# Attention's scores with its products, and its transposes by pairs, in two visits in place of four

## The chip, the cores and the metric

One core of a Trainium2 chip runs the whole program. The metric is the device time of one execution in microseconds, from runs of the same kernel on the chip. The kernel before takes 1135.18 us, the median of 3 runs (1135.1 to 1136.02).

## What is computed

Three stages stand behind each other. Attention has 4 batches, 8 heads, 576 tokens, 64 elements a head, and a window of 128 tokens. Its output, 2304 tokens of 512, goes through a dense layer of 2048 (softplus), and then through a mixture of 8 experts, two for each token.

```python
scores = scale * np.matmul(q, k.transpose(0, 1, 3, 2))
mask = (rel >= 0) & (rel < window)            # window 128
scores = np.where(mask, scores + bias[None], -1000000000.0)
attn = np.exp(scores - np.max(scores, axis=-1, keepdims=True))
attn = attn / (np.sum(attn, axis=-1, keepdims=True) + 1e-09)
x = np.matmul(attn, v)                        # to [2304, 512]
h = x @ w_in
x = (np.maximum(h, 0.0) + np.log1p(np.exp(-np.abs(h)))) @ w_out
# then: top 2 of 8 experts by noisy logits, relu(x @ w1[e]) @ w2[e], weighted sum
```

## The kernel before

**Tiling.** Attention works on 20 units u, five in each batch, of 128 query tokens (the fifth has 64). A unit has 4 head pairs; head pair m runs from 0 to 79 over all units (u = m // 4). The keys of a unit are its own block and the one before, 256 columns where both are there. The dense layer works on 9 chunks of 256 tokens; a chunk needs the products of all units that reach into it.

**The three steps of attention.** `step_a(m0)` (from line 327, scores) makes the scores of head pairs m0 and m0 + 1, that is two pairs of heads: 8 plain f32 matmuls of 64 rows, into two PSUM tiles, one for each of the two heads of a pair. VectorE then adds the bias and reduces each of the four blocks (L350), ScalarE takes the exponential (L356), VectorE the reciprocal of the sums (L361, L362), and GpSimd multiplies by it (L371; early on ScalarE does half of that). The tile "s" has 6 buffers, one for each head pair. The first PSUM tile is free with the third of the four reductions, the second with the fourth. `step_b(m)` (from L378) transposes the weights of one head pair on TensorE (4 transposes into one PSUM tile, L201) and copies them to "pT", on VectorE for an even m (L400), on ScalarE for an odd one (L398). `step_c(m0)` (from L405, products with values) makes the products of two head pairs, 16 plain f32 matmuls into one PSUM tile; ScalarE copies them out rounded (L430), VectorE takes the rest (L435), into the chunk's "xh" and "xl". Below, A, B and C stand for these three steps.

**PSUM.** A, B and C all take their tiles by `ps_t` (L182) from one ring with the tag "t" of 4 slots: two for A, one for each B, one for C. While the second layer's sums of chunk 1 are open (their tiles are called "z"), `few_t` (L176) sets `nt` to 2: z holds two slots and the ring has two. `part_evac` of chunk 1 gives them back.

**The dense layer between.** `mm1` makes one group of 128 of the 2048 for a chunk, 12 matmuls into "h"; softplus takes ScalarE, VectorE and GpSimd; three jobs later `mm2` makes 6 matmuls into "y" (or "z"). Both are rounded-f32 matmuls (L190). A weight is converted on the way, by ScalarE, VectorE and GpSimd (`w_convert`), its load issued by SP.

**What sets the order.** All engines take their instructions in the order in which they are written. TensorE's order is written out by hand; the other engines' instructions are set in by a planner (`Order`) with a cost for each. The lead-in calls `attn_step` for the steps below `attn_until(0)` before the first job. Then each job t calls `side_work` (L1310) twice, behind `mm1` and behind `mm2`: these calls are the gaps. `pieces_of(c)` (L1297) yields the pieces that chunk c + 1 needs, and `side_work` takes so many of them that `fed` reaches `total * gap // gaps`. A chunk of 6 jobs has 10 such gaps; chunk 1 is made in the first three jobs, chunk 2 in the next nine with 16 gaps. What is left is done when the next chunk begins. Step s gives A(s) for an even s, B(s - 3), and for an odd s C(s - 5). Loads of q and k for unit u + 2 stand ahead of step 4u + 1, that of v for unit u ahead of step 4u.

Of the kernel before, what the change touches and what calls it, by code (L numbers as in the profile page):

```python
# [25 lines left out]
class Order:  # L26
# [60 lines left out]
    def mark(self, key):  # L87
        self.done(key, self.now)
# [24 lines left out]
def moe_chain_kernel(ctx, tc, qk, v, w_in, w_out, w_gate, w_noise, noise, w1, w2, out):  # L113
# [160 lines left out]
    NM = 4 * NU  # L274
# [32 lines left out]
    def attn_load_v(u):  # L307
        b, i, q0, nq = units[u]
        r = U[u] = {}

        def load():
            r["v"] = tl(att, [P, H, D], F32, "rawv", 3, ("ce", 4 * min(NU - 1, u + 1) + 3))
            SP.dma_start(r["v"][:nq], v[b, q0:q0 + nq])
        dma(load, ("rawv", u))
# [63 lines left out]
    def step_b(m):  # L378
        u, hp = divmod(m, 4)
        b, i, q0, nq = units[u]  # L380
        m_ = M[m]
        need(("a", m))
        blocks = key_blocks(u)[0]
        nb = len(blocks)
        pt = ps_t(("b", m, len(blocks) - 1 if nq < P else 0), idle="y").rearrange("p (h b t) -> p h b t", h=2, b=2)
        for j in range(2):
            for kb, (c0, nk, vu) in enumerate(blocks):
                tr(pt[:nk, j, kb, :nq], m_["s"][:nq, j, c0:c0 + nk], ident[:nq, :nq])
        mark(("be", m))
        ph = tl(att, [P, 2, 2, P], F32, "pT", 4, ("ce", m))  # L390
        if nb == 2 and blocks[0][1] == blocks[1][1]:
            parts = [(slice(0, P), slice(0, 2))]
        else:
            parts = [(slice(0, blocks[kb][1]), slice(kb, kb + 1)) for kb in range(nb)]
        for x, (pp, kb) in enumerate(parts):
            w = 2 * nq * (kb.stop - kb.start)
            if m % 2:
                ev = ("A", ca(w), lambda pp=pp, kb=kb: ACT.activation(ph[pp, :, kb, :nq], pt[pp, :, kb, :nq], AF.Copy))  # L398
            else:
                ev = ("V", cv(w), lambda pp=pp, kb=kb: DVE.tensor_copy(ph[pp, :, kb, :nq], pt[pp, :, kb, :nq]))  # L400
            chain(ev + (("b", m, x),))
        m_["nb"] = len(parts)
        m_["pT"] = ph
# [35 lines left out]
        del M[m0], M[m0 + 1]  # L439

    LB, LC = 3, 4

    def attn_step(s):
        u = s // 4
        if s % 4 == 1 and u + 2 < NU:
            attn_load_qk(u + 2)
        if s and s % 4 == 0 and u < NU:
            attn_load_v(u)
        pieces = []
        if s < NM and s % 2 == 0:  # L450
            pieces.append(lambda: step_a(s))
        if 0 <= s - LB < NM:
            pieces.append(lambda: step_b(s - LB))
        if 0 <= s - LC - 1 < NM and (s - LC) % 2:
            pieces.append(lambda: step_c(s - LC - 1))
        return pieces

    def attn_last(c):
        return max(u for u in range(NU) if units[u][0] * S + units[u][2] < CT * (c + 1))

    def attn_until(c):
        return 4 * attn_last(c) + 3 + LC + 1

# [829 lines left out]
    NT = len(jobs)  # L1295

    def pieces_of(c):  # L1297
        for s in range(attn_until(c), attn_until(c + 1)):
            yield from attn_step(s)

    starts = {0: (0, NLEAD), NLEAD: (1, 2 * NA - NLEAD)}
    for c in range(2, NCH):
# [2 lines left out]
    feed, fed, total, gap, gaps = None, 0, 0, 0, 1  # L1305
# [37 lines left out]
    for t in range(NT + max(L2, len(items) + 2)):  # L1343
# [11 lines left out]
        if t in starts:  # L1355
            c, n = starts[t]
            if feed is not None:
                for p in feed:
                    p()
            feed = pieces_of(c) if c + 1 < NCH else None  # L1360
            total = 2 * (attn_until(c + 1) - attn_until(c)) if feed else 0
            fed, gap, gaps = 0, 0, 2 * n - 2
        if t == last_start - (NF - NA):
            open_p2()
# [7 lines left out]
        if t < NT:  # L1372
            c, fc = jobs[t]
# [17 lines left out]
        if 0 <= t - L2 < NT:  # L1391
            c, fc = jobs[t - L2]
# [74 lines left out]
```

## Time and profile before

| | us |
|---|---|
| median of 3 runs | 1135.18 |
| the profiled execution | 1135.73 |
| its span, first to last instruction | 1134.0 |
| TensorE busy | 1072.4 |
| VectorE busy | 723.6 |
| ScalarE busy | 616.8 |
| GpSimd busy | 581.7 |

The profile is one execution. PE is TensorE, DVE VectorE, ACT ScalarE, POOL GpSimd, SP SyncE, which issues most of the DMAs; SPq is its queue. PEclk is the granted clock of TensorE as a share of full speed: 1.00 is 2.4 GHz, 0.50 is 1.2 GHz. A row of the timeline merges like instructions that follow each other: its start, its length, engine, line, operation, out<-in, how many, and in brackets the idle time of the engine before it with what ended it. Starts are exact; the ends of matmuls are modelled, so spacings are read from start to start.

### The profile page before, as it was taken

To read this page: it belongs to the slowest core of one execution; us is meant where nothing else is said; L and a number is where in the kernel's file an instruction comes from. 1 tells how busy PE (TensorE), PEld (TensorE's weight loads), DVE (VectorE), ACT (ScalarE), POOL (GpSimd) and SP (SyncE) were. 2 spreads that over 40 slices of the span, in tenths; PEclk is the share of its full clock that TensorE was granted. 3 is DMA by queue.
4 is the path that set the end of the run, shared out by engine and by line. 5 is a ranking of instruction groups with operands and counts; after the bars stand their busy time and mean duration, and the time that the engine had idled before them with its cause. 6 is when DMAs were issued, how large, how long until landed. Compare 5 with 4: busy or idle time off the path is not lost.

```text
span 1134.0 us, 21375 instructions
## 1 busy us (share of the span) xinstructions
PE 1072.4 (95%) x7021; PEld 913.2 (81%) x7021; DVE 723.6 (64%) x1946; ACT 616.8 (54%) x1459; POOL 581.7 (51%) x933
## 2 busy tenths in 40 slices
PE   5599999999999999999998997999999999999997
PEld 3377777777789888888887796997997997999984
DVE  8975788889764666666767685653653653665520
ACT  7876768877764444444453543553553553555521
POOL 4576779889886676777775232222222223222112
PEclk8899999999999999999998998999999999999999
DMA  7231553555683322211348729788888888888723
GB/s 306 102 93 57 182 183 118 196 209 176 204 302 124 102 75 75 76 51 62 122 140 304 239 28 337 207 234 262 223 234 264 228 228 253 250 227 233 213 57 38
DMA packets 96561, 198.94 MB, mean 175 GB/s; under 512 B 34048, under 2 KB 44800, under 8 KB 96448
## 3 DMA queue, kind: packets, MB, share of 16 engines
q1 hardware_dynamic: 86112, 176.01, 47.3%
q0 software_dynamic: 10336, 21.54, 9.7%
q8 instruction: 56, 0.92, 0.4%
q14 instruction: 57, 0.47, 0.2%
HBM read 157.82 MB, written 39.69 MB: 174 GB/s over the span
## 4 chain that ended last, share of the span: by engine, by line
PE 65%; DVE 4%; DMA 4%; POOL 3%; ACT 2%; issue 2%; SPq 1%; DVEq 0%; POOLq 0%; ACTq 0%
PE h L190 31%; PE y L190 21%; PE z L190 9%; PE t L201 3%; PE t L190 1%; DMA rawp<-in_moe_w 1%; POOL sl L555 1%; POOL su L555 1%; DVE wlo L1154 1%; DMA rk<-rect 1%; ACT s L356 1%; DMA raw<-in_moe_w_out 1%; DVE gl L587 0%; DMA out<-ys,rc 0%; DMA x1buf<-x 0%
## 5 line engine op out<-in xcount | busy, mean ns | idle before, releaser
L190 PE MATMUL h<-xh,w 128*128 128x256 f32 x1152 | 239.6, 291 | 5.0 <-DVE sl L583 5.0
L1264 POOL DMA_INDIRECT out<-ys,rc x41 | 83.7, 2042 | 272.3 <-DVE ys L1273 131.6
L1154 DVE TENSOR_TENSOR wlo<-rawp,whi 128x1024 fp32r<-128x1024 f32 x107 | 130.8, 1222 | 136.2 <-ACT whi L1156 129.9
L190 PEld LDWEIGHTS h<-xh,w 128*128 128x128 f32 x1152 | 191.2, 193 | 19.2 <-DVE sl L583 9.5
L1156 ACT ACTIVATE whi<-rawp 128x1024 fp32r<-128x1024 f32 x107 | 113.4, 1060 | 151.2 <-PE h L190 108.1
L555 POOL TENSOR_TENSOR su<-sa,su 128x128 f32<-128x128 f32 x288 | 137.2, 497 | 86.1 <-DVE su L588 73.0
L190 PE MATMUL y<-w,gh 128*128 128x512 f32 x552 | 179.8, 407 | 0.0
L190 PE MATMUL h<-xh,whi 128*128 128x256 f32 x576 | 165.5, 287 | 6.4 <-DVE gl L1203 6.4
L190 PE MATMUL h<-xl,w 128*128 128x256 f32 x576 | 164.4, 285 | 1.1 <-DVE xl L435 1.1
L190 PE MATMUL h<-xl,whi 128*128 128x256 f32 x576 | 163.3, 283 | 0.0
L190 PE MATMUL h<-xh,wlo 128*128 128x256 f32 x576 | 163.2, 283 | 0.0
L580 ACT ACTIVATE sa<-h 128x256 f32<-128x256 f32 x144 | 54.8, 381 | 152.7 <-PE h L190 99.6
L555 POOL TENSOR_TENSOR sl<-sl,su 128x128 f32<-128x128 f32 x288 | 134.5, 488 | 3.9 <-DVE sl L583 2.8
L190 PEld LDWEIGHTS h<-xh,whi 128*128 128x128 f32 x576 | 110.1, 191 | 14.0 <-DVE gl L1203 6.8
L190 PEld LDWEIGHTS h<-xl,whi 128*128 128x128 f32 x576 | 110.2, 191 | 7.1 <-issue 1.4
L190 PEld LDWEIGHTS h<-xl,w 128*128 128x128 f32 x576 | 111.4, 193 | 4.5 <-DVE xl L435 1.6
L190 PEld LDWEIGHTS h<-xh,wlo 128*128 128x128 f32 x576 | 110.2, 191 | 0.0
L190 PE MATMUL y<-w,gl 128*128 128x512 f32 x276 | 108.7, 394 | 0.0
L190 PEld LDWEIGHTS y<-w,gh 128*128 128x128 f32 x552 | 95.3, 192 | 16.3 <-issue 2.7
L371 POOL TENSOR_TENSOR s<-s,st 128x256 f32<-128x256 f32 (+2 forms) x144 | 91.9, 661 | 25.6 <-DVE st L362 14.0
L1063 POOL DMA_INDIRECT xg<-x1buf,rc x41 | 43.2, 1054 | 106.6 <-DVE rc L1052 60.4
L587 DVE TENSOR_TENSOR gl<-sl,gh 128x256 fp32r<-128x256 f32 x144 | 76.6, 533 | 13.3 <-ACT gh L585 10.5
(256 smaller groups left out, 2265.0 us busy)
## 6 DMA issues: line engine op xcount, KB each, us to landing
rawp<-in_moe_w SPq DMA_DIRECT2D x140, 512.0 KB
raw<-in_moe_w SPq DMA_DIRECT2D x44, 512.0 KB
qkT<-in_qk SPq DMA_DIRECT2D x20, 512.0 KB
raw<-in_moe_w_in SPq DMA_DIRECT2D x16, 512.0 KB
raw<-in_moe_w_out SPq DMA_DIRECT2D x16, 512.0 KB
out<-zero SPq DMA_DIRECT2D x19, 256.0 KB
xspill<-xh SPq DMA_DIRECT2D x9, 512.0 KB
xspill<-xl SPq DMA_DIRECT2D x9, 512.0 KB
```

The costliest lines, as they stand in the source:

```text
L190: PE.matmul(o, l, r, start=start, stop=stop)
L201: PE.transpose(o, i, idn)
L356: ACT.activation(s[:nq, j, :n], s[:nq, j, :n], AF.Exp, bias=st[:nq, 0, y], scale=-1.0, accum_out=st[:nq, 1, y])
L371: POOL.tensor_tensor(s[:nq, j, :n], s[:nq, j, :n], st[:nq, 3, 2 * x + j:2 * x + j + 1].to_broadcast([nq, n]), OP.mult)
L555: POOL.tensor_tensor(o[:, z], x[:, z], y[:, z], op)
L580: chain(("A", ca(CT), lambda: ACT.activation(a, ph, AF.Abs)), ("A", ca(CT), lambda: ACT.activation(a, a, AF.Exp, scale=-1.0), ("e", t)), ( ...
L587: ("V", cv(CT), lambda: DVE.tensor_sub(gl, l, f32(gh)), ("g", t)))
L1063: POOL.indirect_dma_start(out=x, out_offset=None, in_=x1buf[:T - 3 * CT if g < NEARLY else TPAD, :], in_offset=bass.IndirectOffsetOnAxis(a ...
L1154: DVE.tensor_sub(lo, t, f32(hi))
L1156: chain(("A", ca(1024), lambda: ACT.activation(hi, t, AF.Copy), None, (("r2", j),)), ("V", cv(1024), low, ("w2", j)))
L1264: POOL.indirect_dma_start(out=out[:, :], out_offset=bass.IndirectOffsetOnAxis(ap=rc[:, a, 0:1], axis=0), in_=ys, in_offset=None, compute_o ...
```

## The change

The feeder's pieces are made anew. One piece, `products(s)`, now does A(s) and then all C up to head pair s - 6, and after that the loads that stood ahead of steps s and s + 1. The other piece does all B up to s - 3, which are two of them. So for two head pairs the feeder has two pieces in place of four (A, B, B, C). `sofar` keeps how far B and C have come. `attn_until(c)` is larger by 2 for every chunk but the first, since C of the same pairs is one step later; `pieces_of` goes by two steps, and `total` counts half as many pieces. The lead-in still goes by `attn_step`, whose pieces are now always two or three, some of them without work.

```diff
     LB, LC = 3, 4
-
-    def attn_step(s):
+    sofar = [0, 0]
+
+    def loads(s):
         u = s // 4
         if s % 4 == 1 and u + 2 < NU:
             attn_load_qk(u + 2)
         if s and s % 4 == 0 and u < NU:
             attn_load_v(u)
+
+    def b_upto(m):
+        while sofar[0] <= min(m, NM - 1):
+            step_b(sofar[0])
+            sofar[0] += 1
+
+    def c_upto(m):
+        while sofar[1] <= min(m, NM - 1):
+            step_c(sofar[1])
+            sofar[1] += 2
+
+    def attn_step(s):
+        loads(s)
         pieces = []
         if s < NM and s % 2 == 0:
             pieces.append(lambda: step_a(s))
-        if 0 <= s - LB < NM:
-            pieces.append(lambda: step_b(s - LB))
-        if 0 <= s - LC - 1 < NM and (s - LC) % 2:
-            pieces.append(lambda: step_c(s - LC - 1))
+        pieces.append(lambda: b_upto(s - LB))
+        pieces.append(lambda: c_upto(s - LC - 1))
         return pieces
+
+    def products(s):
+        if s < NM:
+            step_a(s)
+        c_upto(s - 6)
+        loads(s)
+        loads(s + 1)
+
+    def attn_pieces(s):
+        return [lambda: products(s), lambda: b_upto(s - 3)]
 
     def attn_until(c):
-        return 4 * attn_last(c) + 3 + LC + 1
+        return 4 * attn_last(c) + (10 if c else 8)
...
     def pieces_of(c):
-        for s in range(attn_until(c), attn_until(c + 1)):
-            yield from attn_step(s)
+        for s in range(attn_until(c), attn_until(c + 1), 2):
+            yield from attn_pieces(s)
...
-            total = 2 * (attn_until(c + 1) - attn_until(c)) if feed else 0
+            total = attn_until(c + 1) - attn_until(c) if feed else 0
```

## Rows read from the trace of the kernel before

**Rows 1.** The page's head: the span.
```profile
span 1134.0 us, 21375 instructions
```

**Rows 2.** Windows: stretch, length, engines' busy us (instructions), PEclk, DMA share, GB/s.
```profile
41.00:72.00 31.00, 23.56 (x181) 17.82 (x178) 28.58 (x80) 24.89 (x71) 21.74 (x32) 0.84 0.36 127
72.00:132.00 60.00, 57.21 (x441) 46.29 (x440) 37.78 (x143) 41.68 (x138) 39.15 (x81) 1.00 0.34 111
132.00:305.00 173.00, 166.28 (x1278) 131.54 (x1277) 151.93 (x447) 134.59 (x419) 151.58 (x264) 0.98 0.51 175
305.00:1134.00 829.00, 805.74 (x5013) 704.27 (x5011) 470.15 (x1168) 384.71 (x746) 351.28 (x525) 0.99 0.61 180
```

**Rows 3.** TensorE's waits, 88 to 305 us: total us, times, longest.
```profile
PE t L190 <- ACT pT L398: 2.3, 1, 2.3
PE t L201 <- DVE st L350: 2.3, 2, 1.3
PE t L190 <- DVE st L350: 2.2, 2, 1.4
PE t L201 <- POOL s L371: 1.4, 3, 0.7
```

**Rows 4.** TensorE's timeline, 209 to 217 us: start, us, instruction, shapes, count.
```profile
209.06 0.28 PE L190 MATMUL h<-xl,w 128*128 128x256 f32 x1
209.18 0.28 PE L190 MATMUL h<-xh,w 128*128 128x256 f32 x1
209.29 0.63 PE L190 MATMUL y<-w,gh 128*128 128x512 f32 x2
...
212.00 0.28 PE L190 MATMUL h<-xh,w 128*128 128x256 f32 x1
212.21 1.08 PE L339 MATMUL t<-qkT 64*64 64x256 f32 x8
...
215.63 1.09 PE L190 MATMUL t<-pT,rawv 128*64 128x128 f32 x16
216.66 0.39 PE L190 MATMUL h<-xh,w 128*128 128x256 f32 x1
216.88 0.28 PE L190 MATMUL h<-xl,w 128*128 128x256 f32 x1
```

**Rows 5.** TensorE's timeline where products are followed by scores, 222 us.
```profile
222.72 1.09 PE L190 MATMUL t<-pT,rawv 128*64 128x128 f32 x16
223.75 0.71 PE L339 MATMUL t<-qkT 64*128 64x128 f32 x8
```

**Rows 6.** TensorE's timeline, transposes behind scores with two slots, 98 and 127 us.
```profile
98.64 1.13 PE L339 MATMUL t<-qkT 64*128 64x256 f32 x8
101.07 0.63 PE L201 MATMUL t<-ident,s 128*128 128x128 f32 x4 [1.30 <-DVE st L350]
...
127.68 0.63 PE L201 MATMUL t<-ident,s 128*128 128x128 f32 x4 [0.96 <-DVE st L350]
```

**Rows 7.** VectorE's timeline behind the scores of 98.64 us: first and third reduction.
```profile
99.80 0.42 DVE L350 CUSTOM_DVE_ANT_0 s<-t,relh 128x256 f32<-128x256 f32 x1 [0.63 <-PE t L339]
...
100.49 0.42 DVE L350 CUSTOM_DVE_ANT_0 s<-t,relh 128x256 f32<-128x256 f32 x1
```

**Rows 8.** TensorE's timeline, the products that waited for a copy, and the next scores.
```profile
168.86 0.44 PE L190 MATMUL t<-pT,rawv 128*64 128x128 f32 x4 [2.33 <-ACT pT L398]
...
171.15 2.08 PE L339 MATMUL t<-qkT 64*128 64x256 f32 x8
```

**Rows 9.** Windows of 5 us in which the granted clock was low.
```profile
170.00:175.00 5.00, 5.00 (x24) 3.75 (x24) 4.00 (x15) 3.87 (x15) 4.95 (x9) 0.66 0.10 42
225.00:230.00 5.00, 4.04 (x36) 3.01 (x35) 4.04 (x19) 4.30 (x17) 5.00 (x10) 0.85 0.94 352
230.00:235.00 5.00, 5.00 (x36) 3.94 (x34) 4.93 (x14) 3.37 (x12) 3.13 (x8) 0.81 0.22 90
```

**Rows 10.** SP's own queue, 72 to 305 us: waits of the loads of v.
```profile
SPq L313 <- PE t L190: 39.9, 5, 11.6
```

## The prediction

> **What bounds the kernel now.** I read the page first for the span [rows 1], then the stretches of the run [rows 2]. TensorE is busy nearly all of the time from 72 us on. In 41 to 72 us it is not: VectorE is the full engine there (28.6 of 31 us). The changed code runs from 42 us to about 304 us, where attention's work for the next chunk is threaded between the first layer's matmuls ("h") and the second layer's ("y", for a while "z"). In 132 to 305 us TensorE idles only 6.7 of 173 us, VectorE and GpSimd being 88% busy [rows 2]. After 305 us nothing of the change runs; that stretch waits on its own work and moves as one block with whatever is won or lost before.
>
> So two things count: what TensorE does beside useful columns at the edges of attention's visits, and its waits. Its list of waits for 88 to 305 us [rows 3] holds transposes waiting for GpSimd's normalised scores (1.4 us), products waiting for the copied transposes (2.3), and transposes or products waiting for VectorE's reductions of the scores, that is for a free PSUM slot (2.3 and 2.2).
>
> **Edges.** Attention's scores (A) and products with values (C) are plain f32 matmuls. In the PE timeline [rows 4] an h matmul follows an h matmul after 0.12 us and y follows h after 0.11, but scores follow h after 0.21; behind products the first h takes 0.22 to its successor. So a run of A or C between other work costs about 0.10 at each end, 0.20 in all. Where products are followed directly by scores [rows 5] the products take 1.03 us up to the scores, as they do up to h [rows 4] (216.66 less 215.63, from the same listing), so A and C side by side share one run. How many runs there are follows from the feeder: a chunk's pieces are spread over gaps by integer division. Before, four visits per two pairs of heads come in the order A, B, B, C (B: transposes), in 10 gaps for 16 pieces (24 in two chunks). After, 8 (12) pieces: A with C, then both B. Writing both sequences out from the code, I get 57 runs of A or C behind the third h group before and 32 after: 25 fewer, 25 x 0.20 = 5.0 us. In 14 of the old runs scores meet transposes; I count that end at half, an estimate: 14 x 0.05 = 0.7 less. **Term 1: -4.3 us** (bounds -5.0 and 0).
>
> The Trainium skill speaks against this term ("TensorE: Matmul & The Clock Gate", Step-by-step: what each phase is for): the draining of one matmul overlaps the filling by the next, so that a stream is spaced by its columns. The trace agrees from h to y and not from h to A.
>
> **The stretch with two PSUM slots.** Between the z tiles' first use (about 87.7 us) and their copy (about 133 us) attention has two slots in place of four. Scores take both, so whatever takes a slot next waits for VectorE. Before, that is a B directly behind A, twice: 1.30 us and 0.96 us [rows 6]. VectorE starts its reductions 0.03 us after the last score matmul, and the third, which frees the first slot, starts 0.69 us after the first and ends a little before the transposes start [rows 7]. In the other old visits an h or y group covers this. After, C stands directly behind A in every product visit, and by the feeder's arithmetic five such visits (A 28 to 36 with C 22 to 30) fall into this stretch. What is queued behind the waiting C on TensorE is the next h or y and with it ScalarE's first pass over h; nothing else covers it. I take 1.2 each, between the two rows: 6.0 less the 2.3 that goes. **Term 2: +3.7 us** (bounds 5 x 0.96 - 2.3 = +2.5, and 5 x 2.3 - 2.3 = +9 if VectorE is a conversion step behind, the longest wait on the list).
>
> **Longer lead.** A pair's transposes now come 2.5 pair periods behind its scores, not 1.5. GpSimd's normalisation gets that much longer, so the 1.4 us of waits go; with them goes the low clock behind them, 0.85 and 0.81 granted over two stretches of 5 us [rows 9], 5 x 0.15 + 5 x 0.19 = 1.7 us. **Term 3: -3.1 us** (bounds -3.1 and 0).
>
> Products now have an h or y group and A (1.0 us) between them and their pair's second B, where some had 1.4 us and one more B. The 2.33 us wait for ScalarE's copy at 168.86 [rows 8] has ScalarE standing behind a late weight conversion, which the change doesn't touch, but the copy moves ahead of it. The scores after that wait took 2.08 us, at a granted clock of 0.66 in the stretch [rows 8, 9]: 5 x 0.34 = 1.7. I count half of 2.3 + 1.7. **Term 4: -2.0 us** (bounds -4.0 and +2, since another wait can meet the same late copy).
>
> Waits of C for reductions with four slots (2.2 us, [rows 3]) came about 2.4 us behind A. Now C no longer needs the slot of its own visit's scores; the second B does, behind C, an h or y group and one B, about 3.0 us. **Term 5: -1.0 us** (bounds -2.2 and +2).
>
> **What comes in exchange.** Reductions and the copies of the products stand in one burst on VectorE, and in one chunk two visits hold A, C and both B together, where the second B comes 1.5 us behind A, just what the reductions took on a free VectorE and more than they leave on a full one: 0.5 us each. VectorE and GpSimd do the same work in a shorter time: 152 us in some 165, 92%. A wait of one more engine queue, 1.5 us in all, is my estimate from the sum of the small waits now listed. **Term 6: +2.5 us** (bounds 0 and +8, where all gains come back as waits).
>
> **The start.** In the lead-in the steps are called one by one with the same lags, so nothing moves; empty pieces only let the weight conversion look once more. Up to the second chunk's first h group one more A and one more pair of B are to be done (about 1.3 us of TensorE, and four short reductions), taken from later. VectorE is full there; but transposes wait there for GpSimd too. I take 0 (bounds -2.5 and +1.5).
>
> **Loads.** The loads of q, k and v are still one unit and two units ahead of their use, now in the same visit behind A and C. On SP a load of v waits for old products on TensorE (39.9 us in five cases [rows 10]), with weight loads and spills queued behind it. It is emitted behind the same C as before, q and k right behind v instead of one visit later. I cost this at nothing: the products use v two visits on. If that cover goes, the price is a conversion's late weights, as in term 4.
>
> **Sum.** -4.3 + 3.7 - 3.1 - 2.0 - 1.0 + 2.5 = -4.2 us. The profiled execution took 1135.73 us (span 1134.0 and 1.7 around it), 0.55 above the median of 1135.18. From the median: **1131.0 us**.
>
> **The rivals.**
> 1. All waits named in terms 3 to 5 vanish and none comes: -4.3 + 3.7 - 3.1 - 4.0 - 2.2 = -9.9, 1125.3 us. For it speaks the longer lead everywhere; against it that these waits came from queues that other work fills.
> 2. VectorE and GpSimd become the bound: the gains reappear as waits on reductions, "sl" and "s". Term 6 is +6 to +8, the time 1134.5 to 1136.5. For: 88% busy now, GpSimd full in one of the 5 us stretches [rows 9]. Against: VectorE has a tenth of the stretch left even then, and TensorE idles so little there now.
> 3. Slower: the two slots. If VectorE is behind at each A, the wait is 2.3 us, not 1.2, and costs the clock too: of the waits seen, 1.30 left the clock full and 2.33 didn't, so the mechanism decides between these two. 5 x (2.3 + 1.7) - 2.3 = +17.7 in place of +3.7: 1145 us. Against: VectorE is 63% busy in 72 to 132 us [rows 2].
> 4. An edge between kinds costs nothing, what is seen being the end of a modelled matmul: term 1 is 0, and the change does on TensorE nothing of what it reorders for: +0.1, 1135.3 us. The page cited above would have it so. Against: starts, not ends, carry the 0.21.
>
> **How the numbers follow.** Forecast 0.48 (its own range 1127 to 1135), rival 1 0.14, rival 2 0.14, rival 3 0.16, rival 4 0.08. About 0.2%, 2.3 us, is what a measurement of this kernel can tell from no change. Faster than 1132.9: 0.8 of the forecast (0.38), all of rival 1, a little of rival 2 (0.03): 0.55. Slower than 1137.5: rival 3 and about a quarter of rival 2 and of the forecast's upper end: 0.20. The rest, 0.25, is the same. The range leaves out the low end of rival 1 and most of rival 3: 1123 to 1140.
>
> **What would show it.** Runs of A and C: scores next to products in the PE timeline, each A with C about 2.3 us from edge to edge. Term 2: five waits of C for reductions between 88 and 133 us, 1 to 1.3 us each; if there are none, or if they are over 2 us, the term is wrong. Term 3: no transposes waiting for "s" on GpSimd behind 72 us. Term 4: no product waiting for "pT". Term 6: more idle time of TensorE for reductions or "sl" than now. If the 829 us behind 305 us change in length by over 1 us, the block doesn't move as one, and the forecast fails for a reason not in it.

## The result

The changed kernel takes 1146.87 us, the median of four runs (1146.31 to 1147.63), the kernel before 1135.6 in four runs. The ratio is 1.0105 [1.0088, 1.0121]: slower by 11 to 12 us, where 1131.0 was forecast and 1140 was the end of the range. The profiled execution took 1146.31 us; its span stands against [rows 1], its stretches against [rows 2]. The page's head, kernel after:

```profile
span 1144.5 us, 21362 instructions
```

Windows of the kernel after (columns as in [rows 2]):

```profile
72.00:132.00 60.00, 53.77 (x417) 43.71 (x416) 35.04 (x131) 39.63 (x130) 39.75 (x82) 1.00 0.33 104
132.00:305.00 173.00, 160.89 (x1229) 130.60 (x1230) 148.56 (x438) 129.89 (x407) 144.97 (x251) 0.95 0.50 171
305.00:1144.00 839.00, 815.05 (x5088) 712.34 (x5086) 477.00 (x1182) 390.73 (x763) 355.35 (x537) 0.99 0.61 180
```

TensorE is idle 6.2 us in 72 to 132 us (before 2.8), and 12.1 us in 132 to 305 (before 6.7), and in the latter its granted clock is 0.95 in place of 0.98. VectorE is less busy than before in both (35.0 and 148.6 us for 37.8 and 151.9), GpSimd as busy in the first (39.8 for 39.2) and less in the second (145.0 for 151.6); part of this is that the kernel after, being late, has done less by 305 us. What TensorE waits for, in 75 to 135 us and then in 135 to 310 us of the kernel after (columns as in [rows 3]):

```profile
PE t L190 <- DVE st L350: 7.6, 5, 2.4
...
PE t L190 <- DVE pT L400: 4.8, 3, 1.9
PE t L339 <- DVE xl L435: 3.2, 1, 3.2
PE t L201 <- DVE st L350: 1.8, 2, 1.5
PE t L201 <- POOL sl L577: 0.6, 1, 0.6
```

Against [rows 3] no wait is put down to GpSimd's "s" any more. The 0.6 us that transposes wait for "sl" (at 235.92) is probably one all the same: they read nothing of "sl", and GpSimd finished two multiplications of "s" directly ahead of it (233.93 to 235.41). Products (L190 into t) wait five times for a slot, three times for copies on VectorE, and once the scores (L339) wait.

Where the time is lost can be read from the starts of the h groups, which are the same work in the same order in all kernels of this study. The table gives how much later than in the kernel before each stretch made its kernel; the marks in the kernel before are the 4th h group at 71.2 us, the 19th at 147.6, the 25th at 179.2, the 48th at 305.6, and the end of the span at 1134.0. The two-slot stretch lies in the second column.

| kernel | to 4th h | to 19th | to 25th | to 48th | to the end | sum | that run's time, us | median | ratio to before |
|---|---|---|---|---|---|---|---|---|---|
| after | +2.0 | +3.4 | +2.7 | +0.6 | +1.9 | +10.6 | 1146.3 | 1146.9 | 1.0105 [1.0088, 1.0121] |
| e1 pads stored later | +1.5 | +3.4 | -3.7 | +2.6 | +1.7 | +5.4 | 1141.1 | 1139.6 | 1.0037 [1.0023, 1.0051] |
| e2 the same, kernel before | +1.9 | 0.0 | -2.9 | +1.4 | -2.6 | -2.2 | 1133.5 | 1134.7 | 0.9996 [0.9984, 1.0008] |
| e3 C ahead of A | +6.4 | +3.7 | +2.9 | +6.8 | +1.4 | +21.2 | 1156.9 | 1160.2 | 1.0235 [1.0213, 1.0256] |
| e4 A, C apart with two slots | +1.7 | +0.3 | +0.8 | -3.6 | +0.8 | 0.0 | 1135.8 | 1139.9 | 1.0054 [1.0034, 1.0073] |
| e5 e1 and e4 | +1.5 | +0.3 | -3.7 | +2.6 | +1.5 | +2.3 | 1138.1 | 1136.1 | 1.0010 [0.9998, 1.0021] |
| e6 e5, old start | +0.6 | +2.3 | -3.7 | +2.4 | +1.6 | +3.2 | 1139.0 | 1139.7 | 1.0046 [1.0033, 1.0059] |
| e7 e5, C two head pairs later | +1.4 | +0.3 | -0.4 | -4.7 | -1.6 | -5.0 | 1130.7 | 1133.0 | 0.9985 [0.9975, 0.9996] |
| e8 e1, A, C apart | +1.5 | +0.3 | -2.7 | -2.2 | +2.1 | -1.1 | 1134.6 | 1131.6 | 0.9971 [0.9959, 0.9982] |
| e9 copies on ScalarE | -3.2 | +3.4 | -0.9 | -3.3 | -1.8 | -5.8 | 1130.0 | 1132.1 | 0.9981 [0.9967, 0.9995] |
| e10 A, C apart | +0.8 | +0.3 | -2.3 | -3.1 | -1.7 | -6.0 | 1129.9 | 1132.3 | 0.9974 [0.9964, 0.9983] |
| e11 e8, C two head pairs later | +1.9 | +0.3 | +2.0 | -5.3 | +0.2 | -1.0 | 1134.7 | 1134.6 | 0.9990 [0.9981, 1.0000] |
| e12 A, B, B, C, same lags | +1.5 | +1.3 | -1.1 | +0.8 | -0.5 | +2.0 | 1137.7 | 1137.4 | 1.0017 [1.0004, 1.0029] |
| e13 before, copies on ScalarE | -0.9 | +0.9 | +1.3 | +3.5 | -1.7 | +3.0 | 1138.8 | 1139.9 | 1.0039 [1.0025, 1.0054] |
| e14 e10, copies on ScalarE | -0.4 | +1.3 | -2.3 | -5.4 | +0.6 | -6.1 | 1129.6 | 1129.0 | 0.9934 [0.9921, 0.9948] |
| e15 A with C, B one by one | +1.8 | +3.1 | +2.7 | -3.7 | -0.9 | +3.0 | 1138.7 | 1140.3 | 1.0054 [1.0037, 1.0072] |
| e16 e14, A with C from chunk 4 on | -0.9 | +0.9 | -0.8 | -3.3 | -2.4 | -6.5 | 1129.2 | 1131.3 | 0.9964 [0.9951, 0.9978] |

The stretches are of one profiled run each, the ratios of all runs; where the two differ (e3, e4 and e8, by 3 us or more) the ratio decides. The stretch to the end moves by -2.6 to +2.1 though none of the changed code runs there, so two kernels' sums can lie over 4 us apart without a cause. The stretch to the 4th h group is of the same kind: e2 has the order of the kernel before up to there and is 1.9 us late, at a granted clock of 0.66 in 68 to 73 us (before 1.00). Of the +2.0 of the kernel after, 0.8 is there at 22.5 us already (21.7 before), in the lead-in, and e10 with the same lead-in doesn't have it; the rest is about the 1.3 us of scores and transposes that it does early.

### The profile page after: what moved, and what is told of

The parts are those of the page before. It is cut to its first block, busy times and chain, and to the rows that moved or that the text cites. A ratio compares the mean times of both kernels' runs of the same rounds, so it can differ in the third digit from the quotient of the medians.

```text
span 1144.5 us, 21362 instructions
## 1 busy us (share of the span) xinstructions
PE 1074.6 (94%) x7021; PEld 918.1 (80%) x7021; DVE 724.7 (63%) x1946; ACT 616.4 (54%) x1459; POOL 578.9 (51%) x933
## 4 chain that ended last, share of the span: by engine, by line
PE 77%; DVE 12%; POOL 3%; issue 2%; DMA 2%; ACT 2%; SPq 1%; DVEq 0%; POOLq 0%; ACTq 0%
PE h L190 35%; PE y L190 23%; PE z L190 9%; PE t L201 4%; PE t L190 3%; DVE s L350 2%; PE t L339 2%; DVE cva L519 1%; DVE cva L518 1%; DVE gl L609 1%; POOL sl L577 1%; DVE cva L517 1%; DVE w L533 1%; DVE su L610 1%; POOL su L577 1%
## 5 line engine op out<-in xcount | busy, mean ns | idle before, releaser
L190 PE MATMUL h<-xh,w 128*128 128x256 f32 x1152 | 238.5, 290 | 6.1 <-DVE sl L605 6.1
L190 PEld LDWEIGHTS h<-xh,w 128*128 128x128 f32 x1152 | 190.8, 193 | 18.1 <-DVE sl L605 11.2
L190 PE MATMUL y<-w,gh 128*128 128x512 f32 x552 | 179.6, 407 | 0.0
L190 PE MATMUL h<-xh,whi 128*128 128x256 f32 x576 | 165.6, 288 | 6.5 <-DVE gl L1225 6.5
L190 PE MATMUL h<-xl,w 128*128 128x256 f32 x576 | 164.1, 285 | 1.2 <-DVE xl L435 1.2
L190 PE MATMUL h<-xl,whi 128*128 128x256 f32 x576 | 163.4, 284 | 0.0
L190 PE MATMUL h<-xh,wlo 128*128 128x256 f32 x576 | 163.4, 284 | 0.0
L190 PEld LDWEIGHTS h<-xh,whi 128*128 128x128 f32 x576 | 110.4, 192 | 14.2 <-DVE gl L1225 6.9
L190 PEld LDWEIGHTS h<-xl,whi 128*128 128x128 f32 x576 | 110.4, 192 | 7.1 <-issue 1.4
L190 PEld LDWEIGHTS h<-xl,w 128*128 128x128 f32 x576 | 111.3, 193 | 4.5 <-DVE xl L435 1.4
L190 PEld LDWEIGHTS h<-xh,wlo 128*128 128x128 f32 x576 | 110.4, 192 | 0.0
L190 PE MATMUL y<-w,gl 128*128 128x512 f32 x276 | 109.2, 396 | 0.6 <-DVE gl L609 0.6
L190 PEld LDWEIGHTS y<-w,gh 128*128 128x128 f32 x552 | 95.8, 192 | 15.0 <-issue 1.7
L356 ACT ACTIVATE s<-s,st 128x256 f32<-128x256 f32 (+2 forms) x160 | 76.0, 477 | 21.8 <-DVE st L350 21.7
```

What stands on the lines that cost most here:

```text
L190: PE.matmul(o, l, r, start=start, stop=stop)
L356: ACT.activation(s[:nq, j, :n], s[:nq, j, :n], AF.Exp, bias=st[:nq, 0, y], scale=-1.0, accum_out=st[:nq, 1, y])
```

## Where the time went in the kernel after

**The slots.** TensorE's timeline, kernel after: scores, and behind them the products of the same visit, with two PSUM slots (the first and the last of the five):

```profile
95.36 1.14 PE L339 MATMUL t<-qkT 64*128 64x256 f32 x8
97.80 0.66 PE L190 MATMUL t<-pT,rawv 128*64 128x128 f32 x8 [1.30 <-DVE st L350]
...
129.95 1.08 PE L339 MATMUL t<-qkT 64*64 64x256 f32 x8
133.41 0.84 PE L190 MATMUL t<-pT,rawv 128*64 128x128 f32 x11 [2.38 <-DVE st L350]
```

VectorE's timeline at the same two places, kernel after: the third reduction, which frees the first slot, and at the second place the conversion and the first reduction too.

```profile
97.22 0.42 DVE L350 CUSTOM_DVE_ANT_0 s<-t,relh 128x256 f32<-128x256 f32 x1
...
131.41 0.82 DVE L519 SCALAR_TENSOR_TENSOR cva<-raw,cva 128x512 int32<-128x512 int32 x1
132.16 0.41 DVE L350 CUSTOM_DVE_ANT_0 s<-t,relh 64x256 f32<-64x256 f32 x1
...
132.84 0.41 DVE L350 CUSTOM_DVE_ANT_0 s<-t,relh 64x256 f32<-64x256 f32 x1
```

At 95.36 VectorE is free when the scores end, and the wait is 1.30 us all the same, as in the first four of the five: three reductions in a row, then the slot. At 129.95 VectorE is in a weight conversion, the reductions begin at 132.16, and the wait is 2.38.

**The late load.** SP's queue waits in 150 to 180 us, kernel after, the one that counts:

```profile
SPq L266 <- DVE pad L263: 13.9, 1, 13.9
```

SP's timeline behind that wait, kernel after:

```profile
166.36 1.79 SPq L266 DMA_DIRECT2D rect<-pad  x4
168.25 0.39 SPq L313 DMA_DIRECT2D rawv<-in_v  x1
168.69 0.45 SPq L304 DMA_DIRECT2D qkT<-in_qk  x1
169.19 0.43 SPq L505 DMA_DIRECT2D raw<-in_moe_w_in  x1
```

ScalarE's timeline, where it waits for that load, kernel after:

```profile
175.60 0.66 ACT L509 ACTIVATE cva<-raw 128x512 f32<-128x512 f32 x1 [5.92 <-DMA raw<-in_moe_w_in]
...
176.47 0.37 ACT L430 ACTIVATE xh<-t 128x256 fp32r<-128x256 f32 x1
```

TensorE's timeline, where the scores of the next visit wait, kernel after:

```profile
177.40 2.07 PE L339 MATMUL t<-qkT 64*128 64x256 f32 x6 [3.23 <-DVE xl L435]
179.41 1.12 PE L190 MATMUL t<-pT,rawv 128*64 128x128 f32 x8
```

Read them upward. Scores wait for a slot that holds old products; these products are copied by ScalarE (L430) and VectorE (L435); ScalarE stands 5.92 us in its queue for a weight that SP issued at 169.19; and SP had stood 13.9 us in front of four small stores ("pad") whose data VectorE made late, and then issued v and q, k ahead of the weight.

The order behind the stores is the change's own doing. In e10 (below), where A and C are apart, SP issues the weight directly behind them, as it does before (161.77) and in e12 (164.76). SP's timeline, e10:

```profile
160.09 1.80 SPq L266 DMA_DIRECT2D rect<-pad  x4
161.93 0.44 SPq L517 DMA_DIRECT2D raw<-in_moe_w_in  x1
162.47 0.40 SPq L313 DMA_DIRECT2D rawv<-in_v  x1
```

ScalarE then waits 3.99, 1.80 and 4.37 us for the weight (before, e10, e12), and 5.92, 5.33 and 6.38 us in the kernel after, e4 and e15, where v and q, k go first. In e9 they go first too, with a wait of 3.78.

**The copies.** TensorE's timeline, kernel after, at the first of three places where products wait for VectorE's copy of the transposes:

```profile
196.09 1.13 PE L339 MATMUL t<-qkT 64*128 64x256 f32 x8
198.81 1.09 PE L190 MATMUL t<-pT,rawv 128*64 128x128 f32 x16 [1.59 <-DVE pT L400]
```

VectorE's timeline ahead of that copy, kernel after:

```profile
195.25 0.44 DVE L517 TENSOR_SCALAR cva<-cva 128x512 f32<-128x512 f32 x1
...
196.33 0.98 DVE L519 SCALAR_TENSOR_TENSOR cva<-raw,cva 128x512 int32<-128x512 int32 x1
197.24 0.83 DVE L609 TENSOR_TENSOR gl<-sl,gh 128x256 fp32r<-128x256 f32 x1
197.99 0.68 DVE L400 COPY pT<-t 128x512 f32<-128x512 f32 x1
```

The copy stands behind a conversion and a pass of softplus. The h or y group and the 1.0 us of A that lie between the pair's last transposes and its products don't cover that burst.

**The clock.** Windows of 5 us behind these waits, kernel after (the third figure from the end is PEclk):

```profile
133.00:138.00 5.00, 4.59 (x42) 4.24 (x43) 3.54 (x12) 4.24 (x15) 2.91 (x6) 1.00 0.41 117
175.00:180.00 5.00, 2.60 (x12) 1.77 (x14) 3.19 (x7) 4.40 (x15) 1.24 (x3) 0.70 0.85 346
180.00:185.00 5.00, 5.00 (x26) 3.99 (x23) 4.97 (x17) 4.88 (x15) 4.77 (x9) 0.62 0.38 153
236.00:241.00 5.00, 5.00 (x18) 3.34 (x18) 2.71 (x8) 4.34 (x16) 4.26 (x11) 0.50 0.22 89
300.00:305.00 5.00, 5.00 (x29) 4.20 (x26) 3.69 (x10) 2.07 (x7) 3.93 (x7) 0.67 0.46 150
```

The granted clock is 0.70 and 0.62 around the 3.23 us wait, 0.50 (1.2 GHz) over a whole window behind a 1.28 and a 0.60 us wait at 233.73 and 235.92, 0.67 behind one of 1.95 at 299.10, but 1.00 behind 2.38 at 133.41.

**The balance** up to the 48th h group: the start +2.0 (of which some 1.3 is work done early), more idle time +3.4 and +5.4, the clock 173 x 0.03 = +5.2, together 16.0 - 1.3 = +14.7. Found: +8.7. So about 6 us were won as well, of which the edges are the larger part (below). The clock is known to two digits only, so this closes to 2 us.

## The experiments

Two accounts were open. In the first, three separate things cost the time, each with its own remedy: the late load, the two slots, the start. In the second it is the joining itself: with A directly ahead, C has its slot and its copies too late, and what is seen at each place is the form that this takes there.

**e1 and e2: the late load.** The four stores of "pad" go to SP seven jobs later, in the kernel after (e1) and in the kernel before (e2).

```diff
+        pads.append(pad)
+    def store_pads():
...
-            SP.dma_start(r.rearrange("(p n) z -> p (n z)", p=P), pad.rearrange("p n z -> p (n z)"))
+            SP.dma_start(r.rearrange("(p n) z -> p (n z)", p=P), pads[0].rearrange("p n z -> p (n z)"))
...
+        if t == 27:
+            store_pads()
```

> The changed kernel, with the four stores of the pad tile issued at job 27 and not at job 20, where SP stands 13.9 us for VectorE's pad operation and the next weight load lands late. Theory A (the extra time is a sum of separate waits, of which the late load is one): ScalarE's wait of 5.9 us for the load goes, TensorE's 3.2 us for the scores' slot behind it too, and the low clock after it (0.70 and 0.62 over 5 us each, 3.4 us): 4 to 6.6 us less, 1140 to 1143. Theory B (VectorE is simply too full, a wait removed comes back at the next place): less than 1.5 us, 1145.5 to 1147.

> The kernel before with the same move of the four stores. Theory A: its own event of this kind goes, 2.33 us of wait and 1.7 us of clock, so up to 4 us less: 1131.5 to 1134. Theory B: within 1 us of 1135.6.

e1 gives back 7.3 of the 11.3 us by the medians, a little more than was expected, and the scores' wait of 3.23 is gone. Its waits, 72 to 305 us:

```profile
PE t L190 <- DVE st L355: 7.6, 5, 2.4
...
PE t L190 <- ACT sa L608: 2.2, 1, 2.2
```

(The lines stand 5 further down in this kernel.) The five waits for slots are what they were, and products now wait 2.2 us elsewhere. In the kernel before, the same edit removes the 2.33 us wait of [rows 8], but transposes wait 1.60 and 0.66 us at 198.86 and 173.73 in its place, and the time is the same: what was expected to be gained there was not. So the stores where they were cost the kernel after, and moving them gains the kernel before nothing.

**e4, e5, e6: the slots, both, and the start.** In e4 A and C are two pieces, with a gap between them, only for the chunks that are made while there are two slots. e5 is e4 with e1's stores. e6 is e5 with the feed of the first three jobs as it was.

```diff
+    def attn_apart(s):
+        return [lambda: scores_only(s), lambda: c_and_loads(s), lambda: b_upto(s - 3)]
...
-            yield from attn_pieces(s)
+            yield from (attn_apart(s) if c in (1, 2) else attn_pieces(s))
...
+            if c in (1, 2):
+                total = total * 3 // 2
```

> The changed kernel with A and C as two pieces while chunks 2 and 3 are made (where the two-slot stretch lies), B still by pairs. Theory A: the five waits of C behind A (7.6 us) go, up to 10 runs of f32 matmuls more are to be paid at 0.20: 5 to 6 us less, 1141 to 1142, with the later stretches as they were. Theory B: the waits come back as scores and transposes waiting for copies in the same stretch, less than 2 us in all.

> Both single edits together: the pad stores at job 27, and A and C as two pieces while chunks 2 and 3 are made. Alone they took 7.3 us (to 1139.6) and 7.0 us (to 1139.9) from the changed kernel. Theory A (the extra time is a sum of separate waits): the gains add, 1132 to 1134. Theory B (one lateness of VectorE that shows wherever TensorE is ahead): they overlap, 1137 to 1139.

> The run with both edits, and the first three jobs fed in the old order too (A, B and B, C, with the old lags), so that the longer lead begins with chunk 2. Theory A: at the fourth h group the changed kernel was 1.95 us behind, of which this gives back 1.5 to 2.5: 1.5 to 2.5 us under the run with both edits. Theory B: VectorE is full there in either order; what isn't done then is paid later, within 0.7 us of it.

With A and C apart the five waits for reductions are gone; transposes wait 1.01 and 1.65 us for copies instead, and the stretch costs +0.3 us in place of +3.4. That is what the slots were worth: 3 us. e4's four runs spread from 1135.8 to 1142.8 us; its ratio is 0.5% below that of after. e5, both remedies at once, gives back 10.8 of 11.3 us, less than 7.0 and 7.3 together, and lies between the two ranges that were expected. So the first account explains how to get back to the kernel before, not how the forecast's gain could have come. e6 missed: with the old feed the start costs +0.6 and not +1.5, but +2.3 follows in place of +0.3 (products wait 1.30 us for a slot at 105.53 again), and it ends 3.6 us above e5. The start is not a loss of its own.

**e10, e8, e7, e11: room between A and C.** e10 is the changed kernel with A and C apart for all chunks but the first two, nothing else. e8 is the same with e1's stores. e7 is e5, but from chunk 4 on (counted from 0) C stays joined and comes two head pairs further behind A, with the loads of v two steps later; e11 is e8 with that lag. First e10's edit (the loads go with C), then the piece that e7 adds.

```diff
-            yield from attn_pieces(s)
+            yield from (attn_apart(s) if c else attn_pieces(s))
```

```diff
+    def products_later(s):
+        if s < NM:
+            step_a(s)
+        c_upto(s - 8)
+        loads(s, 2)
+        loads(s + 1, 2)
```

> The changed kernel with the one edit that A and C are two pieces from chunk 2 on; the pad stores stay at job 20. Theory A (joining A with C is what costs, by the two slots and by C's waits for copies): most of the 11.3 us go; with the pad stores moved too it was 1131.6; without that the late load still holds ScalarE once, 2 to 4 us: 1133 to 1136. Theory B (the gain of the run with both edits was the pads'): 1138 to 1140.

> Pad stores at job 27, and A and C as two pieces for all chunks from 2 on; in the run with both edits that is so for chunks 2 and 3 only. So 22 runs of f32 matmuls more from chunk 4 on. Theory A (an edge costs what the timeline shows): 22 x 0.20 = 4.4 us more than the run with both edits, less what C's waits for copies lose, since an h or y group now stands between A and C as well (up to 4 us): 0 to +4.5 us; h and y groups beside attention keep their 0.1 us at each edge. Theory B (edges cost nothing): the same or less than the run with both edits by what the waits lose, -4 to 0 us.

> The run with both edits, and from chunk 4 on C one pair of head pairs later still (C up to s - 8, loads of v two steps later), so that the copies to pT have a whole period. Theory A (C waits for copies that stand behind weight conversion on VectorE): the three waits of C for pT behind 150 us (4.8 us) and the low clock behind two of them (about 3 us) go, one more wait may come elsewhere: 4 to 7 us under the run with both edits, 1126 to 1130. Theory B (VectorE is too full): the waits return as waits for reductions or for sl, less than 1.5 us.

> A and C apart from chunk 2 on, pad stores at job 27, and from chunk 4 on C a pair of head pairs later. With C at the nearer place 1131.6. Theory A (C's copies are late): the remaining wait of this kind (1.5 us at 295 us) goes, 1129.5 to 1131.5. Theory B (the distance between A and C already gives the cover): within 0.7 us of 1131.6, or worse for the last chunks being done later.

e10 takes away 14.6 us and is faster than the kernel before, with the stores where they were; e8 is no different from it. So the late load is not a cause apart from the joining: in e10 SP stands 10.9 us for the same stores, but the weight goes ahead of v and q, k, ScalarE waits 1.80 us for it, and no wait of TensorE in 150 to 210 us is longer than 0.39. What the room is worth beside the late load is seen from e1, where ScalarE doesn't wait for that weight either: e8 is 8.0 us faster. e8 lies 4.5 us below e5, where 0 to +4.5 was expected if edges cost 0.20 and -4 to 0 if they cost nothing. That doesn't make edges free: e8 has 17 runs of A or C more than e5 in the trace (22 were expected), but in 132 to 305 us TensorE idles 5.3 us in place of 9.2, and the granted clock is 1.00 in place of 0.96. The window of e10:

```profile
132.00:305.00 173.00, 168.78 (x1299) 134.81 (x1300) 153.75 (x444) 132.51 (x414) 152.56 (x265) 1.00 0.53 179
```

The two largest waits of e10, 72 to 305 us:

```profile
PE t L201 <- DVE pT L400: 2.6, 2, 1.7
PE t L190 <- DVE pT L400: 1.5, 1, 1.5
```

The clock is full again and TensorE idles 4.2 us, less than before's 6.7. e7 shows the same from another side: still joined, but with copies two head pairs older, products never wait for VectorE's copies in 132 to 305 us, and it too is a little faster than before, 3.1 us under e5 where 4 to 7 were expected. (A new wait of scores for a copy, 2.96 us at 221.96, has come.) Both together, e11, missed what was expected: it loses 3 us against e8. Up to the 25th h group it falls 5 us behind e8, of which it wins 3 back up to the 48th; why is not shown.

**e3: the order turned round.** C ahead of A in the same visit, so that C needs no slot of A's.

```diff
     def products(s):
+        c_upto(s - 6)
         if s < NM:
             step_a(s)
-        c_upto(s - 6)
```

> The changed kernel with C ahead of A in a visit. Theory A: in the two-slot stretch no C waits for reductions any more (five waits, 7.6 us); instead the scores' second tile waits for the products' copies, 0.5 to 0.9 us each as at 107 us of the kernel before, so about 4 us less there. With four slots C loses the 1.0 us of cover that A gave it: its waits for the copied transposes (4.8 us in three) grow by 3 us or more. Time 1143 to 1148. Theory B (the burst on VectorE is what costs): the burst is the same, the waits for the copies don't grow, 1142 to 1144.

Its waits, 72 to 305 us, the two largest:

```profile
PE t L190 <- DVE pT L400: 12.1, 8, 3.2
PE t L201 <- DVE st L350: 3.5, 3, 1.6
```

No product waits for a reduction any more, and the kernel is 1.3% slower still: 1160.2 us, where neither account expected more than 1148. The four us that were to come back in the two-slot stretch did not (+3.7 for +3.4): scores wait for copies there in place of products for reductions. And 1.0 us less between transposes and products makes eight waits for VectorE's copies of three; at the start, too, products wait for copies (four waits of 1.1 to 2.5 us, +6.4). So beside the slots C lacks the copies.

**e12 and e15: which of the two joinings.** The same lags as in the kernel after, A and C or the two B taken apart or not. e15 joins A with C and takes B one by one (`attn_three`); e12 joins nothing (`attn_four`). e12 also puts C behind the two B, as before, where e10 has it directly behind A's gap; so e12 differs from both its neighbours in the table below by that order too.

```diff
+    def attn_three(s):
+        return [lambda: products(s), lambda: b_upto(s - 4), lambda: b_upto(s - 3)]
+    def attn_four(s):
+        return [lambda: scores_only(s), lambda: b_upto(s - 4), lambda: b_upto(s - 3), lambda: c_and_loads(s)]
```

> The changed kernel's lags (B a pair later, C with it) with four pieces from chunk 2 on: A, B, B, C, as before. It differs from the kernel before by the longer lead and by the first three jobs, and from the changed one by nothing being joined. Theory A (the longer lead by itself is good): the waits of transposes for GpSimd behind 132 us (1.4 us) and the low clock behind them are gone, the start costs about 2 us, the late load stays: 1133 to 1137. Theory B (the longer lead is what puts TensorE out of step with the late loads): 1139 or more.

> The changed kernel's A with C in one visit, B one by one, from chunk 2 on. Theory A (joining A with C costs by itself): the five waits with two slots stay, and C's waits for copies; nothing joined was 1137.4, so 1144 to 1149. Theory B (only both joinings together cost, by their burst): 1136 to 1141.

| ratio to before | B one by one | B by pairs |
|---|---|---|
| A and C apart | e12 1.0017 | e10 0.9974 |
| A with C | e15 1.0054 | after 1.0105 |

Two steps of the table change one thing: joining A with C costs 1.3% where B comes by pairs (e10 to after), and taking B by pairs costs 0.5% where A and C are joined (e15 to after). The steps to and from e12, 0.4% each, hold the other place of C as well. So the two halves of the change work against each other in the joined order; I read it so that pairs of transposes bring pairs of copies, and joined products want both copies one group and 1.0 us later; no run isolates that. e15 was expected at 1144 to 1149 us if joining A with C costs by itself, and at 1136 to 1141 if only both joinings together do; it took 1140.3, in the second range, 3 us above e12. e15's waits in 72 to 305 us have the same two kinds:

```profile
PE t L190 <- DVE st L350: 7.4, 5, 2.2
PE t L190 <- ACT pT L398: 6.4, 4, 4.6
PE t L190 <- DVE pT L400: 2.5, 1, 2.5
```

e12 has the longer lead with nothing joined. It was expected at 1133 to 1137 us without the waits of transposes for GpSimd. It took 1137.4, and those waits are there, in 132 to 305 us:

```profile
PE t L201 <- POOL s L371: 1.4, 3, 0.6
```

**e9, e13, e14, e16: the copies made by ScalarE.** If VectorE's burst is the cause, the copies of even pairs on ScalarE should undo it with everything still joined. e9 is that; e13 does it to the kernel before, e14 to e10, and e16 joins A with C again in e14 from chunk 4 on. The edit is in `step_b`:

```diff
-            if m % 2:
+            if m >= 0:
```

> The changed kernel with the copies to pT of even head pairs on ScalarE too, nothing on VectorE. Theory A (C waits because its copy stands behind weight conversion and the burst of reductions in VectorE's queue): the waits on VectorE's copies (4.8 us) and the low clock behind two of them (3.3 us) go; ScalarE takes 40 copies of 0.3 to 0.6 us more and some waits come there: 3 to 6 us under the changed kernel's 1146.9. Theory B (all engines are late by the same work, whichever holds the copy): the waits name ScalarE instead, within 2 us of 1146.9 or above.

> The kernel before with all copies to pT on ScalarE. Theory A (the move helps the changed kernel because its C waits for VectorE's copies): here only the lead-in gains, 4 to 5 us as it did in the changed kernel (its first h group came 4.4 us earlier), and the stretch behind is as now: 1130.5 to 1132. Theory B (VectorE is what holds attention in any order): the stretch behind 72 us gains as much as the changed kernel's did (8 us): 1122 to 1125.

> The changed kernel with A and C apart from chunk 2 on and all copies on ScalarE. Theory A: the lead-in's 4.4 us are gained on top of 1132.3, and one wait for a copy on VectorE (1.5 us): 1126 to 1128.5. Theory B (ScalarE becomes the late one): 1130 or more.

> All copies on ScalarE, A and C apart for chunks 2 and 3 only and joined from chunk 4 on. It has 22 runs of f32 matmuls fewer than the one with A and C apart throughout. Theory A (an edge costs 0.20, and with the copies in time joining gains): 2 to 4.5 us under that one. Theory B (joining costs whichever engine copies): the same or above it.

e9 is 14.8 us faster than the kernel after, where 3 to 6 were expected, and a little faster than before. The five waits for slots are still there (1.30 four times, 1.01), as is their +3.4; what is gained is the start (-3.2 in place of +2.0: VectorE was the full engine there, and the first h group comes at 37.5 us for 41.9, before anything is joined), and 132 to 305 us, where the granted clock is 0.99 and TensorE idles 6.9 us (after 0.95 and 12.1, e10 1.00 and 4.2). Between the 4th and the 48th h group that is 7.5 us less than in the kernel after. e13 missed what was expected: in the old order the same edit is worth 4 to 5 us the wrong way. The two largest waits of e13, 132 to 305 us:

```profile
PE t L190 <- ACT pT L398: 3.7, 1, 3.7
PE t L201 <- POOL s L371: 3.6, 3, 2.5
```

Behind the longest of each the granted clock is 0.66 in 170 to 175 us and 0.68 in 230 to 235. VectorE is busy 135 of the 173 us there (before 152), but products wait 3.7 us for a copy on ScalarE, and the old order's transposes 2.5 us for GpSimd. The move pays in the new order (e9, e14) and not in the old; which part of the new order it needs, the longer lead or the pairs, no run separates. e14, the move with A and C apart, beats both kernels: 1129.0 us, 0.9934, just above the 1126 to 1128.5 expected. Its window:

```profile
132.00:305.00 173.00, 170.42 (x1310) 136.43 (x1308) 146.07 (x418) 142.60 (x449) 153.93 (x267) 1.00 0.54 182
```

TensorE idles 2.6 us of 173. e16 asked whether joining pays once the copies are in time: at 0.9964 it is 3.4 us slower than e14 by the ratios (2.3 by the medians), with products waiting 1.94 us for a copy at 286.23. (It has 17 runs of A or C fewer than e14 in the trace, not 22.) Edges saved by joining A with C don't pay for the room that joining takes from C even then.

## Why the prediction was wrong

The step that failed is the cover of C. Terms 4 and 5 took it as a gain, or at nothing, that C stands directly behind A, with only an h or y group and A between it and the copies that it reads; the paragraph on loads cost their new place at nothing. In its place the runs showed three waits of products for VectorE's copies (4.8 us), a wait of 3.23 us of scores behind a late weight, and low clock behind these, in all 173 x 0.03 = 5.2 us. With A and C apart (e10) the scores' wait and the low clock are gone, and of the products' waits one of 1.5 us is left. The terms one by one:

**Term 1, the edges: right.** TensorE's timeline of a joined visit without a wait, kernel after:

```profile
259.46 0.39 PE L190 MATMUL y<-w,gl 128*128 128x512 f32 x1
259.78 1.14 PE L339 MATMUL t<-qkT 64*128 64x256 f32 x8
260.84 1.09 PE L190 MATMUL t<-pT,rawv 128*64 128x128 f32 x16
261.87 0.39 PE L190 MATMUL h<-xh,w 128*128 128x256 f32 x1
262.09 0.28 PE L190 MATMUL h<-xl,w 128*128 128x256 f32 x1
```

A and C follow each other with no extra start, one edge of 0.10 in front (0.32 where y to y takes 0.23) and one behind (0.22 where h to h takes 0.12). The chunk between the 37th and the 43rd h group, which has full clock in all three, takes 31.7 us before, 31.4 after and 31.2 in e10, with one wait of 1.39, of 1.48 and of 0.31: without it 30.4, 29.9 and 30.8, with 8, 4 and 8 runs of A or C. So a run less is worth 0.24 us against e10 and 0.12 against the old order, around the 0.20 of the sum; in all the traces count 58 runs before and 32 after (57 and 32 in the prediction), 26 fewer, 3 to 6 us. The balance above left about 6. Rival 4 falls with it. The Trainium skill's statement cited there ("TensorE: Matmul & The Clock Gate", Step-by-step: what each phase is for), that the drain of one matmul overlaps the fill of the next, so that a stream is spaced by its columns, does not hold at these edges: the rows, before and after, show 0.10 us at each.

**Term 2, the two slots: right in kind, too small.** Five waits, as counted. Forecast at 1.2 each, they were 1.30 four times and 2.38 once: 7.6 - 2.3 = +5.3 for the +3.7 of the sum, inside its bounds. Rival 3's time, 1145 us, is near the measured one, but not by its mechanism: it wanted +17.7 from five waits of 2.3 us with the clock low behind each; one was so long, and the clock behind it was 1.00.

**Term 3, longer lead: not borne out.** No wait is put down to "s" any more, but e12 has the same lead and waits 1.4 us for "s" in three times, as much as the kernel before: the lead alone doesn't remove them. The clock's 1.7 us were not won either: 236 to 241 us ran at 0.50, behind waits of products for copies and of transposes for GpSimd. e10 has full clock there and makes -3.1 between the 25th and the 48th group, the size of the term, but other waits changed in it as well.

**Term 4, the late copy: the wrong sign.** It held that the copy moves ahead of ScalarE's late conversion. It did, but ScalarE's conversion was later than before (5.92 us of waiting for the weight in place of 3.99) and then held the next thing, the copying out of products, and with it the slot that scores waited for: 3.23 us in place of 2.33, and low clock over 10 us in place of 5 (5 x 0.30 + 5 x 0.38 = 3.4 in place of 1.7). That is +2.6, and the stretch up to the 25th group came out at +2.7, where this term held -2.0. The bound of +2 named this case ("another wait can meet the same late copy"), and was a little too small. The paragraph on loads called the loads of q, k and v free: in the new order SP issued two of them ahead of the late weight, and e1 shows that SP's stand decides 7 us in this order.

**Term 5 and the cover of C.** C's waits for reductions with four slots did go, 2.2 us. But term 4's sentence that products have "an h or y group and A (1.0 us)" between them and their last transposes was taken as a gain. It is the cover that failed: three waits for VectorE's copies, 4.8 us, and low clock behind two. The kernel before has no such wait, so its rows priced none; and the burst of a conversion ahead of a copy (at 195.25 to 197.99, 2.7 us) could have been read from VectorE's timeline as a bound. e9, e10 and e7, which take the copy off VectorE, take away the closeness, or give the copy more time, each take away most or all of this.

**Term 6: one part as forecast, the rest not.** Transposes wait for reductions with four slots twice, 1.8 us, about the 0.5 us each in two visits that it held. Its other 1.5 us stood for full engines; VectorE was less busy than before, and GpSimd about as busy; e10 fills both more (153.8 and 152.6 us of 173 in 132 to 305 us) and is faster. Rival 2, which wanted them full, falls.

**The start and the tail.** +2.0 against a bound of +1.5; 0.8 of it lies in the lead-in, ahead of what was moved, and the rest is work done early. Behind the 48th group +1.9, where a block that moves as one was forecast, with over 1 us as the sign that it doesn't: waits of h for VectorE's "sl" went from 0.81 and 0.49 to three of 0.48 to 1.01 us, and one of y for "gl" of 0.59 came. In the other kernels that stretch varies as much in both directions, so it stands without a cause.

**What is shown and what isn't.** Shown: that joining A with C, with transposes by pairs, makes the loss (e10 against the kernel after), and that room for C or copies off VectorE removes it. Not settled: what part of it is SP's new order of loads, which no run changed by itself; how much the place of C behind the two B counts in e12; why the lead of e12 leaves the waits for "s"; and how the gains of e1 and e4 share the part in which they overlap.

## What to carry to other kernels

When two steps of a pipeline are issued together, ask of the second what it waits for (a slot that the first has just taken, a copy from the step before), and whether the work that used to lie between them was its cover; read the longest burst of the engine that makes its input as the price. An edge of 0.1 us on the busy engine is real, but one wait of 1.3 us pays for a dozen. Time the halves of a regrouping apart: here transposes by pairs, with the longer lead and A and C apart, took 0.3% off the kernel before, with the copies moved too 0.7%, while the whole change added 1.0%.

## What the runs showed of the hardware

A consumer that takes a PSUM slot directly behind the scores, with two slots, waited 1.30 us whether it was B or C, in before, after, e9, e13 and e15, where VectorE was free and the scores took 1.13 us: three reductions at a distance of 0.35 us and what lies around them. Where the scores themselves took longer, 1.36 to 1.74 us, it was 0.95 to 1.01 (before, e9, e12). The length of a wait alone did not tell whether the clock falls: 2.38 us at 133.41 left it at 1.00 in the next 5 us, while 1.28 and 0.60 us within 3 us, at 233.73 and 235.92, were followed by a stretch at 0.50. And one kernel's runs lay 1.3 us apart in the kernel after and 7.0 in e4 (1135.8 to 1142.8), four runs each; why is not shown.
